# The second batch's attention state on 120 partitions instead of 80 and 40

## The chip, the core and the metric

The kernel runs on one core of one Trainium2 chip. The metric is the device time of one execution in microseconds (us), the median of several runs. Six engines matter: TensorE (PE, whose weight loads the profile lists as PEld), VectorE (DVE), ScalarE (ACT), GpSimd (POOL) and SyncE (SP), which issues most transfers.

## The reference

Three stages follow one another: a recurrent attention with gates, a dense feed-forward layer, and a feed-forward layer with 8 experts of which each token takes one. The change lies in the first.

```python
# attention: batch 2, heads 8, tokens 768, head size 40
m_new = np.maximum(f_gate[:, :, t] + m, i_gate[:, :, t])
f_stab = np.exp(f_gate[:, :, t] + m - m_new)
i_stab = np.exp(i_gate[:, :, t] - m_new)
C = f_stab[..., None, None] * C + i_stab[..., None, None] * np.einsum('bhd,bhe->bhde', vt, kt)
n = f_stab[..., None] * n + i_stab[..., None] * kt
y[:, :, t] = o * (C @ qt) / max(abs(n @ qt), 1)
# dense layer: 1536 tokens, 320 -> 2048 -> 320
h = x @ w_in;  g = np.maximum(0.01 * h, h);  x = g @ w_out
# experts: argmax of x @ w_gate picks one of 8, with room for 384 tokens each, 320 -> 1024 -> 320
```

## The kernel before

The attention is done in chunks of 128 tokens. There are 12 of them, numbered i: six (j = 0 to 5) for the first batch and six for the second, so the second batch is i = 6 to 11. Inside a chunk each token meets the others by a product of scores and values (`pi`); what came before the chunk reaches it through a state of 40 x 41 numbers a head (41: the value's 40 and the normalizer), which meets the chunk's queries in another product (`pj`). Most products run in fp16, where each operand stands as a high part and a remainder, so that the small parts are not lost.

The steps of a chunk that matter here:

- `cast` puts the queries of a head on 120 columns of `qst`: high part, low part, high part, 40 each; a transposing transfer makes `qT` of it, with these on rows 0 to 39, 40 to 79 and 80 to 119. The keys stand on 120 rows of `kT` too.
- `kw` (att_kw, L332, POOL) multiplies the chunk's keys by their decay, written twice beside each other: 128 partitions x 8 heads x 2 x 40 fp32 numbers.
- `st` (att_state) multiplies `kw` (weights, 80 columns a head, fp32) with the values: `pu`, 8 products (L343), whose 80 rows hold the same state twice. In the trace each shows as two records. POOL multiplies the old state by its decay (`cg`, L350), DVE adds (`cf`, L352; in a batch's first chunk DVE copies, L347), ACT rounds to fp16 (`ch`, L356, 80 partitions: high, high), and the remainder `cl` (L357, 40 partitions) is made by POOL in the first four chunks and by DVE after that. A batch's last chunk makes no state.
- `sc` makes the scores `pS` (L373, products of 120 rows and 128 columns), DVE multiplies them by the decay, ACT and DVE split them in high (`ah`) and remainder (`al`).
- `av` (att_av) makes `pi` (L397 to L399, three products a head, from chunk 4 on; one fp32 product a head, L395, in chunks 0 to 3) and, where the batch has a state already, `pj`: for each head one product of 80 rows (L407: q's high and low with the state's high) and one of 40 rows (L408: q's high with the remainder). DVE scales `pj` (L409) and adds `pi` (L412); `out` divides (POOL, L424) and gates (`y`, L426), ACT and DVE make the two halves of `xr`, POOL cuts a part of it (L440), and SP transposes it to `xT` (L447), the input of the dense layer.

The dense layer works in units: `h` (L586, eight products over 320 inputs, for up to 512 columns), then `t` (ACT L798, DVE L799), `gh` (ACT L800), `gl` (POOL L801), and two units later the products `px` into the 320 outputs (L590 to L592). Its units are the bulk of PE's work while the second batch's attention runs. After it the tokens are routed (`x2r`, `plg`, and so on), gathered and multiplied with the experts' weights (`xe`, `py`), which SP loads (`wa`, `wc`) and ACT and DVE split.

A table of steps (ORDER) sets the order in which the steps are written; for the second batch and the dense layer a scheduler with a model of the engines then sets the order of each engine's queue. Each engine works its queue in order. Products of the attention share two buffers of PSUM (pool psA, tag a); tiles of the attention in SBUF have two buffers each (pool a2).

## Time and profile before

| | |
|---|---|
| median of 3 runs | 424.47 us (424.04 to 424.86) |
| the profiled execution | 424.7 us |
| its span on the core | 423.0 us |
| mean granted clock of TensorE | 0.971 |
| instructions in the profile | 9186 |

The profiled execution lasted 1.7 us longer than its span (424.7 less 423.0), for what lies around the program. Times in the trace are microseconds from the span's start. In a timeline a row is the start, the duration, the engine, the line, the operation with its tiles (out<-in), partitions and shapes, the count, and in brackets the idle time ahead of it with what ended it. Products overlap in PE's pipeline, so a product's cost in a row of products is the distance from its start to the next start, not its duration. In a view of windows each stretch has its length, then busy us and count of PE, PEld, DVE, ACT and POOL, then the granted clock, the share of the DMA engines and GB/s.

### The profile page before, as it was taken

The numbers are of one execution on the slowest core, as the hardware profiler recorded it, in microseconds if no ns is written. First come the engines' busy times: TensorE is split into PE (matmuls) and PEld (weight loads), VectorE is DVE, ScalarE is ACT, GpSimd is POOL, SyncE is SP. The second block draws the span as 40 slices with busy tenths as digits, with TensorE's granted clock in tenths as the row PEclk, the third lists the DMA queues.
The fourth block names the chain that finished last, engine by engine and source line by source line (L and its number), as shares of the span: only waits on it lengthen the run. The fifth ranks groups of instructions, "written<-read, shape, count | busy, mean of one in ns | idle before, by whom it ended". The sixth has DMA issues, their size and how long they took to land. (4 is left out here: it accounts for less than half of the span.)

```text
span 423.0 us, 9186 instructions
## 1 busy us (share of the span) xinstructions
PE 367.9 (87%) x3597; PEld 286.3 (68%) x3597; DVE 300.8 (71%) x516; ACT 227.6 (54%) x440; POOL 170.8 (40%) x207
## 2 busy tenths in 40 slices
PE   0878657889799998999999999798779999789993
PEld 0767547668588875666656666595667898568882
DVE  8998999998669664877563374756689967866121
ACT  4461647427676747555355354751378966765222
POOL 4451651816446562465734373443124212222102
PEclk9999999669989999999999999999899999899999
DMA  9999999757998866099611349996197989722000
GB/s 172 218 296 233 262 246 211 126 108 154 210 191 122 176 153 135 2 240 180 152 43 32 60 158 302 303 238 195 45 218 218 312 223 347 169 63 61 33 17 19
DMA packets 146130, 70.22 MB, mean 166 GB/s; under 512 B 115666, under 2 KB 136692, under 8 KB 146080
## 3 DMA queue, kind: packets, MB, share of 16 engines
q1 hardware_dynamic: 144160, 65.44, 67.2%
q0 software_dynamic: 1920, 4.08, 2.7%
q8 instruction: 35, 0.57, 0.6%
q14 instruction: 15, 0.12, 0.1%
HBM read 43.65 MB, written 13.17 MB: 134 GB/s over the span
## 5 line engine op out<-in xcount | busy, mean ns | idle before, releaser
L586 PEld LDWEIGHTS <-pc 128*128 128x128 f16 x1728 | 117.9, 101 | 34.0 <-issue 11.5
L586 PE MATMUL h<-xT,pc 128*128 128x128 f16 (+3 forms) x768 | 99.6, 282 | 5.0 <-DMA xT<-xr 3.0
L801 POOL TENSOR_TENSOR gl<-t,gh 128x512 f16<-128x512 f32 (+1 forms) x52 | 60.0, 1155 | 63.6 <-ACT gh L800 63.4
L586 PE MATMUL h<-xe,pc 128*128 128x128 f16 x960 | 57.3, 222 | 5.5 <-PEq L940 2.0
L590 PE MATMUL px<-pc,gh 128*128 128x320 f16 x192 | 58.2, 305 | 2.1 <-ACT gh L800 2.1
L901 POOL DMA_INDIRECT out_dram<-ye,ix x24 | 26.7, 1114 | 81.1 <-ACT ye L900 80.1
L591 PE MATMUL px<-pc,gh 128*128 128x320 f16 x192 | 58.2, 305 | 0.0
L592 PE MATMUL px<-pc,gl 128*128 128x320 f16 x192 | 56.3, 306 | 0.6 <-POOL gl L801 0.6
L799 DVE SCALAR_TENSOR_TENSOR t<-h,t 128x512 f32<-128x512 f32 (+1 forms) x52 | 33.4, 644 | 30.0 <-ACT t L798 29.8
L889 DVE SCALAR_TENSOR_TENSOR hl<-h,hh 128x512 f16<-128x512 f32 x48 | 31.3, 685 | 32.4 <-ACT hh L888 32.3
L800 ACT ACTIVATE gh<-t 128x512 f16<-128x512 f32 (+1 forms) x52 | 30.9, 594 | 29.1 <-DVE t L799 28.6
L798 ACT ACTIVATE t<-h 128x512 f32<-128x512 f32 (+1 forms) x52 | 28.9, 555 | 29.5 <-PE h L586 28.9
L499 DVE SCALAR_TENSOR_TENSOR pc<-wa,pc 128x1024 f16<-128x1024 f32 (+1 forms) x36 | 36.9, 1024 | 8.9 <-ACT pc L498 6.8
L590 PE MATMUL py<-pc,hh 128*128 128x320 f16 x120 | 36.6, 305 | 3.1 <-PEq L943 2.3
L888 ACT ACTIVATE hh<-h 128x512 f16<-128x512 f32 x48 | 27.1, 594 | 21.5 <-PE h L586 20.2
L592 PE MATMUL py<-pc,hl 128*128 128x320 f16 x120 | 36.7, 306 | 1.6 <-DVE hl L889 1.5
L498 ACT ACTIVATE pc<-wa 128x1024 f16<-128x1024 f32 (+1 forms) x36 | 29.6, 863 | 15.3 <-DVE wa L483 9.0
L591 PE MATMUL py<-pc,hh 128*128 128x320 f16 x120 | 36.6, 305 | 0.0
L499 DVE SCALAR_TENSOR_TENSOR pc<-wc,pc 128x1280 f16<-128x1280 f32 x20 | 31.4, 1571 | 3.7 <-ACT pc L498 3.5
L498 ACT ACTIVATE pc<-wc 128x1280 f16<-128x1280 f32 x20 | 25.3, 1266 | 2.3 <-DVE wc L483 2.2
L590 PEld LDWEIGHTS <-gh 128*128 128x128 f16 x192 | 19.2, 100 | 10.8 <-ACT gh L800 2.6
L900 ACT ACTIVATE ye<-py,mt 128x320 f32<-128x320 f32 x24 | 12.4, 525 | 26.0 <-PE py L592 11.9
(178 smaller groups left out, 658.5 us busy)
## 6 DMA issues: line engine op xcount, KB each, us to landing
wc<-in_moe_w_dram SPq DMA_DIRECT2D x16, 640.0 KB, 6.5
wa<-in_moe_w_dram SPq DMA_DIRECT2D x16, 512.0 KB, 9.8
raw<-in_moe_w_out_dram SPq DMA_DIRECT2D x4, 1280.0 KB
scr<-zero SPq DMA_DIRECT2D x8, 588.0 KB, 4.4
raw<-in_moe_w_in_dram SPq DMA_DIRECT2D x4, 1024.0 KB
lb<-lam_d SPq DMA_DIRECT2D x8, 512.0 KB, 4.6
wa<-in_moe_w_dram SPq DMA_DIRECT2D x16, 128.0 KB
qkv<-in_k_dram SPq DMA_DIRECT2D x12, 160.0 KB, 2.9
```

Of the source, the lines that this page charges most:

```text
L498: nc.scalar.activation(hi, x, AF.Copy, scale=s)
L499: nc.vector.scalar_tensor_tensor(out=lo, in0=x, scalar=s, in1=hi, op0=ALU.mult, op1=ALU.subtract)
L586: nc.tensor.matmul(ph, lhsT=w, rhs=xT[:, x, 0:ncol], start=(m == 0), stop=(m == len(seq) - 1))
L590: nc.tensor.matmul(py, lhsT=gh, rhs=oh[:, kc, :], start=first, stop=False)
L591: nc.tensor.matmul(py, lhsT=gh, rhs=ol[:, kc, :], start=False, stop=False)
L592: nc.tensor.matmul(py, lhsT=gl, rhs=oh[:, kc, :], start=False, stop=last)
L798: nc.scalar.activation(t, ph, AF.Copy, scale=0.01 * S_G)
L799: nc.vector.scalar_tensor_tensor(out=t, in0=ph, scalar=S_G, in1=t, op0=ALU.mult, op1=ALU.max)
L800: mark[0] = nc.scalar.activation(gh, t, AF.Copy)
L801: nc.gpsimd.tensor_tensor(out=gl, in0=t, in1=gh, op=ALU.subtract)
L888: nc.scalar.activation(hh[:, to[0], to[1]], ph, AF.Relu)
L889: nc.vector.scalar_tensor_tensor(out=hl[:, to[0], to[1]], in0=ph, scalar=0.0, in1=hh[:, to[0], to[1]], op0=ALU.max, op1=ALU.subtract)
```

## The change

For the second batch the state is made three times instead of twice: `kw` holds three copies of the keys (960 numbers a partition instead of 640), a product of `pu` has 120 columns of weights instead of 80, and `cf`, `cg` and `ch` stand on 120 partitions. The remainder is written by DVE over the first 40 partitions of `ch`, so these hold remainder, high, high, against q's high, low, high in `qT`. One product of 120 rows a head then does what two did. The new function `copies` sets which chunks do this: i of 6 and more. The first batch keeps two copies and both products; the tiles are allocated for three copies in both.

```diff
--- before.py
+++ after.py
@@ -255,6 +255,7 @@
 
     NPB = 4
     NPOOL = 4
+    XB = NCH
     blocks = BLOCKS
     block_of = {i: (bi, o) for bi, tl in enumerate(blocks) for o, i in enumerate(tl)}
     xTs = {}
@@ -323,38 +324,50 @@
                                 fill=0.0, base=0, channel_multiplier=-1)
         T["dd", i] = dd
 
+    def copies(i):
+
+        return 2 if i < XB else 3
+
     def att_kw(i):
         b, j = divmod(i, NCH)
         xs = T.pop(("xs", i))
         if j == NCH - 1:
             return
-        kw = a2.tile([P, H, 2, D], F32, tag="kws", name=f"kw{i}")
-        nc.gpsimd.tensor_tensor(out=kw, in0=xs[:, 0].unsqueeze(2).to_broadcast([P, H, 2, D]), op=ALU.mult,
-                                in1=ws[:, j, b * H:(b + 1) * H].unsqueeze(2).unsqueeze(3).to_broadcast([P, H, 2, D]))
+        nr = copies(i)
+        kw = a2.tile([P, H, 3, D], F32, tag="kws", name=f"kw{i}").rearrange("p h r d -> p (h r d)")[:, 0:H * nr * D]
+        kw = kw.rearrange("p (h r d) -> p h r d", h=H, r=nr)
+        nc.gpsimd.tensor_tensor(out=kw, in0=xs[:, 0].unsqueeze(2).to_broadcast([P, H, nr, D]), op=ALU.mult,
+                                in1=ws[:, j, b * H:(b + 1) * H].unsqueeze(2).unsqueeze(3).to_broadcast([P, H, nr, D]))
         T["kw", i] = kw
 
     def att_state(i):
         b, j = divmod(i, NCH)
         if j == NCH - 1:
             return
-        pu = psA.tile([2 * D, H, D1], F32, tag="a", name=f"pu{i}")
+        nr = copies(i)
+        pu = psA.tile([nr * D, H, D1], F32, tag="a", name=f"pu{i}")
         kw = T.pop(("kw", i))
         for h in range(H):
             nc.tensor.matmul(pu[:, h, :], lhsT=kw[:, h].rearrange("p r d -> p (r d)"), rhs=T["qkv", i][:, 1, h, :],
                              start=True, stop=True)
-        cf = a2.tile([2 * D, H, D1], F32, tag="cf", name=f"cf{i}")
+        cf = a2.tile([3 * D, H, D1], F32, tag="cf", name=f"cf{i}")[0:nr * D]
         if j == 0:
             nc.vector.tensor_copy(cf, pu)
         else:
-            cg = a2.tile([2 * D, H, D1], F32, tag="cg", name=f"cg{i}")
+            cg = a2.tile([3 * D, H, D1], F32, tag="cg", name=f"cg{i}")[0:nr * D]
             nc.gpsimd.tensor_tensor(out=cg, in0=T.pop(("cf", i - 1)), op=ALU.mult,
-                                    in1=dk[0:2 * D, j, b * H:(b + 1) * H].unsqueeze(2).to_broadcast([2 * D, H, D1]))
+                                    in1=dk[0:nr * D, j, b * H:(b + 1) * H].unsqueeze(2).to_broadcast([nr * D, H, D1]))
             nc.vector.tensor_tensor(out=cf, in0=pu, in1=cg, op=ALU.add)
         T["cf", i] = cf
-        ch = a2.tile([2 * D, H, D1], F16, tag="ch", name=f"ch{i}")
-        cl = a2.tile([D, H, D1], F16, tag="cl", name=f"cl{i}")
+        ch = a2.tile([3 * D, H, D1], F16, tag="ch", name=f"ch{i}")[0:nr * D]
         nc.scalar.activation(ch, cf, AF.Copy)
-        lo_eng(i).tensor_tensor(out=cl, in0=cf[0:D], in1=ch[0:D], op=ALU.subtract)
+        if nr == 3:
+
+            cl = None
+            nc.vector.tensor_tensor(out=ch[0:D], in0=cf[0:D], in1=ch[0:D], op=ALU.subtract)
+        else:
+            cl = a2.tile([D, H, D1], F16, tag="cl", name=f"cl{i}")
+            lo_eng(i).tensor_tensor(out=cl, in0=cf[0:D], in1=ch[0:D], op=ALU.subtract)
         T["cs", i] = ch, cl
 
     def lo_eng(i):
@@ -404,6 +417,9 @@
             ch, cl = T.pop(("cs", i - 1))
             pj = psA.tile([P, H, D1], F32, tag="a", name=f"pj{i}")
             for h in range(H):
+                if cl is None:
+                    nc.tensor.matmul(pj[:, h, :], lhsT=qT[0:KST, h, :], rhs=ch[:, h, :], start=True, stop=True)
+                    continue
                 nc.tensor.matmul(pj[:, h, :], lhsT=qT[0:2 * D, h, :], rhs=ch[:, h, :], start=True, stop=False)
                 nc.tensor.matmul(pj[:, h, :], lhsT=qT[0:D, h, :], rhs=cl[:, h, :], start=False, stop=True)
             nc.vector.tensor_tensor(out=hh, in0=pj,
```

What the scheduler makes of it starts to differ about 131 us into the program, at the second batch's chunk 7 (the first of it that has a state). Three places follow. In these rows a number behind a tile's name tells its copies apart.

TensorE, in the middle of chunk 7's attention products, before (`v1h`, `v1l` are the values' high part and remainder):

```order
L397 LDWEIGHTS ah_1497
L397 MATMUL pi_1561<-v1h_189,ah_1497 128x41
L398 LDWEIGHTS ah_1497
L398 MATMUL pi_1561<-v1l_190,ah_1497 128x41
L407 LDWEIGHTS qT_1436
L407 MATMUL pj_1587<-ch_1453,qT_1436 128x41
L408 LDWEIGHTS qT_1436
L408 MATMUL pj_1587<-cl_1454,qT_1436 128x41
```

and in the changed kernel:

```order
L412 LDWEIGHTS al_1497
L412 MATMUL pi_1560<-v1h_189,al_1497 128x41
L421 LDWEIGHTS qT_1436
L421 MATMUL pj_1586<-ch_1453,qT_1436 128x41
L421 LDWEIGHTS qT_1436
L421 MATMUL pj_1586<-ch_1453,qT_1436 128x41
L421 LDWEIGHTS qT_1436
L421 MATMUL pj_1586<-ch_1453,qT_1436 128x41
```

The 16 products of two heights have become 8 of one; they stand ahead of the second half of `pi`, five and then three, where before all stood together.

TensorE, at the state of chunk 7, before:

```order
L592 LDWEIGHTS gl
L592 MATMUL px_756<-pc_804,gl 128x320
L343 MATMUL pu_1903<-qkv_1424,kw_1896 80x41 x6
L586 LDWEIGHTS pc_268
L586 MATMUL h<-xT_532,pc_268 128x256
```

and in the changed kernel:

```order
L602 MATMUL h<-xT_532,pc_804 128x256
L351 MATMUL pu_1894<-qkv_1424,kw_1887 120x41 x7
L606 LDWEIGHTS gh
L606 MATMUL px_756<-pc_804,gh 128x320
L607 LDWEIGHTS gh
L607 MATMUL px_756<-pc_804,gh 128x320
L386 LDWEIGHTS kT_1847
L386 MATMUL pS_0_1946<-qT_1848,kT_1847 128x128
```

The six and two products of the state have become one and seven, and stand ahead of 12 products `px` that came before them; the scores of chunk 8 have moved forward, to stand behind them.

ScalarE, at the exponentials of two decay matrices (`lb`, L321 before and L322 after), before:

```order
L798 ACTIVATE t<-h 128x512
L321 ACTIVATE lb_1486<-lb_1486,zt 128x128 x8
L288 ACTIVATE v1h_189<-qkv_1898 128x8x40
L800 ACTIVATE gh<-t 128x512
L321 ACTIVATE lb_2072<-lb_2072,zt 128x128 x8
L436 ACTIVATE xr_1759<-y_201,inv_all 128x320
```

and in the changed kernel:

```order
L814 ACTIVATE t<-h 128x512
L322 ACTIVATE lb_1485<-lb_1485,zt 128x128 x2
L452 ACTIVATE xr_1750<-y_201,inv_all 128x320
L289 ACTIVATE v1h_189<-qkv_1889 128x8x40
L322 ACTIVATE lb_2062<-lb_2062,zt 128x128 x8
L816 ACTIVATE gh<-t 128x512
```

A unit's `gh` stood between the two groups of eight exponentials and now stands behind both; `xr` of an earlier chunk, which stood behind both, now stands between them.

## Rows read from the trace of the kernel before

**Rows 1.** The page's first part: busy time, share and instructions of each engine.

```profile
PE 367.9 (87%) x3597; PEld 286.3 (68%) x3597; DVE 300.8 (71%) x516; ACT 227.6 (54%) x440; POOL 170.8 (40%) x207
```

**Rows 2.** Windows: busy PE, PEld, DVE, ACT, POOL, granted clock, DMA share, GB/s.

```profile
131.00:141.00 10.00, 9.73 (x137) 8.23 (x135) 9.70 (x18) 5.99 (x11) 5.14 (x6) 1.00 1.03 163
...
151.00:161.00 10.00, 9.58 (x70) 6.25 (x69) 5.42 (x9) 4.46 (x10) 5.90 (x8) 1.00 0.66 117
161.00:171.00 10.00, 8.91 (x81) 5.45 (x79) 4.41 (x9) 7.21 (x18) 3.89 (x5) 1.00 0.52 118
...
231.00:241.00 10.00, 9.44 (x92) 6.46 (x90) 3.77 (x14) 3.04 (x7) 2.79 (x4) 1.00 0.48 89
...
262.00:275.00 13.00, 10.70 (x93) 7.29 (x92) 8.30 (x10) 8.87 (x15) 4.69 (x5) 1.00 1.03 296
```

**Rows 3.** Groups of PE by line and form: the first products of pj, ten chunks.

```profile
L407 PE MATMUL pj<-ch,qT 80*128 80x41 f16 x80 | 16.0, 200 | 0.0
```

**Rows 4.** Timeline of PE at chunk 8's pi (24 products) and pj (16).

```profile
182.76 0.18 PE L397 MATMUL pi<-v1h,ah 128*128 128x41 f16 x1
...
183.34 0.18 PE L399 MATMUL pi<-v1h,al 128*128 128x41 f16 x1
183.37 0.18 PE L407 MATMUL pj<-ch,qT 80*128 80x41 f16 x1
183.48 0.19 PE L408 MATMUL pj<-cl,qT 40*128 40x41 f16 x1
183.60 0.19 PE L407 MATMUL pj<-ch,qT 80*128 80x41 f16 x1
...
185.23 0.19 PE L408 MATMUL pj<-cl,qT 40*128 40x41 f16 x1
185.35 0.60 PE L586 MATMUL h<-xT,pc 128*128 128x512 f16 x2
```

**Rows 5.** Timeline of PE at a chunk's scores, between products of 128 rows.

```profile
131.39 0.39 PE L373 MATMUL pS<-qT,kT 120*128 120x128 f16 x4
131.61 0.27 PE L586 MATMUL h<-xT,pc 128*128 128x256 f16 x1
```

**Rows 6.** Timeline of PE and PEld at fp32 products of 80 and of 128 columns.

```profile
195.54 1.27 PE L343 MATMUL pu<-qkv,kw 128*80 128x41 f32 x16
196.65 0.60 PE L586 MATMUL h<-xT,pc 128*128 128x512 f16 x2
...
68.98 1.23 PEld L343 LDWEIGHTS pu<-qkv,kw 128*80 128x80 f32 x16
70.25 0.96 PEld L317 LDWEIGHTS pb<-lam,identf 16*128 16x128 f32 x8
...
32.34 3.75 PE L395 MATMUL pi<-qkv,lb 128*128 128x41 f32 x16
35.88 0.24 PE L407 MATMUL pj<-ch,qT 80*128 80x41 f16 x1
```

**Rows 7.** Timeline of POOL at kw of chunk 8, and what follows it.

```profile
153.96 1.26 POOL L332 TENSOR_TENSOR kw<-qkv,ws 128x640 f32<-128x640 f32 x1
155.85 1.16 POOL L801 TENSOR_TENSOR gl<-t,gh 128x512 f16<-128x512 f32 x1 [0.62 <-ACT gh L800]
```

**Rows 8.** Timeline of DVE: additions on 80 and on 128 partitions.

```profile
154.96 0.48 DVE L352 TENSOR_TENSOR cf<-pu,cg 80x328 f32<-80x328 f32 x1
...
141.76 0.49 DVE L412 TENSOR_TENSOR hh<-hh,pi 128x328 f32<-128x328 f32 x1
```

**Rows 9.** Timeline of ACT, POOL, SP and PE: from chunk 7's output to its xT.

```profile
144.71 2.43 ACT L321 ACTIVATE lb<-lb,zt 128x128 f32<-128x128 f32 x8
...
146.41 0.72 POOL L424 TENSOR_TENSOR hh<-hh,dn 128x320 f32<-128x320 f32 x1
...
153.23 1.21 SPq L447 DMA_TRANSPOSE xT<-xr  x1
...
156.10 1.89 PE L586 MATMUL h<-xT,pc 128*128 128x512 f16 x8 [0.42 <-DMA xT<-xr]
```

## The prediction

> **What bounds the kernel now.** I read the page's busy times first, then windows of ten microseconds over the stretch that the change touches, then PE's timeline at the products that change, and last the chain that leads from the attention's output to PE. PE is busy for 87% of the span, ahead of DVE with 71%, ACT with 54% and POOL with 40% [rows 1]. An average could hide that PE waits just here, so the windows decide: from 120 to 262 us, where the second batch's attention runs between the dense layer's units, there are four windows in which PE isn't busy throughout, and those are shown: 0.27, 0.42, 1.09 and 0.56 us of idle time, 2.34 us in 142 [rows 2]. The granted clock is 1.00 in each of these windows, so all distances of this stretch are at the full level of 2.4 GHz. In it PE's queue itself is the limit: a microsecond taken out of it should move nearly all that follows by a microsecond. From 262 us on, where the experts begin, this ends: 10.70 of 13 us [rows 2].
>
> **What is removed: half of the products `pj`.** In chunk 8 the 16 products run from 183.37 to the next unit's `h` at 185.35, 1.98 us or 0.124 us each, without any wait [rows 4]. The 24 products `pi` just ahead of them have as many columns (41) and the same type, yet 23 distances fill 182.76 to 183.34, 0.025 us each [rows 4]. The difference isn't the size. It shows where the height changes: from `pi` (128 rows) to the first product of 80 rows 0.03, from 80 rows to 40 rows 0.11, from 40 back to 80 0.12, from the last of 40 rows to `h` with 128 rows 0.12 [rows 4]. A product of 120 rows stands between products of 128 at no such price: four scores with 128 columns take 0.22 us, from 131.39 to the next `h` at 131.61, 0.055 us each [rows 5]. So I read the 0.124 as the price of a change of height among products of 80, 40 and 128 rows, and expect none of it among 120 and 128. The new eight products then cost between 0.025 each (the pace of `pi`, same 41 columns) and 0.055 (the scores, which have three times the columns); I take 0.025, since the columns are the same. A chunk saves 1.98 less 8 x 0.025, which is 1.78; five chunks of the second batch have such products (7 to 11; the trace's 80 products of 80 rows are eight in each of ten chunks, five of these unchanged [rows 3]), so the sum is 8.9 us, and 7.7 at 0.055.
>
> The Trainium skill, "TensorEngine Tiling (Array Packing)", section "Key Properties", says that changing the tiling mode drains the engine, a change of tile within a mode not. The trace's 0.11 to 0.12 at each change of height [rows 4] agrees with it, and the unpaid step between 120 and 128 rows [rows 5] too; it bears out the reading by heights against the first rival below, whose time would be 422.4 us.
>
> **What is added on PE: wider weights for `pu`.** A product of the state has 120 columns of fp32 weights instead of 80. Each shows as two records, 16 a chunk, and 16 take 1.11 us (195.54 to 196.65), 69 ns each [rows 6]. The weight loads beside them go by columns: 16 loads of 80 columns in 1.23 us are 77 ns each, eight of 128 columns right behind them in 0.96 us are 120 ns each [rows 6], so 48 columns cost 43 ns and 40 columns 36 ns. Five chunks (6 to 10; the last makes no state) have 80 records, 2.9 us in all, on PE's path. The bounds are far apart: nothing, if the load isn't what paces them (a gain is excluded, no column is taken away), and 11.0 us, if they fell to the pace of the fp32 products of 128 columns near the program's start, 16 in 3.54 us (32.34 to 35.88) or 221 ns [rows 6], of which 120 columns are 207: 138 ns more for each of 80. I take 36 ns, because these loads, 69 us into the program, are at the pace that this stretch has, and they stand side by side.
>
> **What is added elsewhere.** POOL's `kw` has half more numbers: 1.26 us for 640 [rows 7], so 0.63 more in each of five, 3.2 us on POOL. What hides it is POOL's idle time: behind `kw` of chunk 8 it waits 0.62 us for ACT before its next `gl` [rows 7], and over the span it is busy for 40% [rows 1]. Uncovered it would delay a `gl` by up to 0.63 us a chunk, and PE has two units in hand before it needs that one. The additions and the rounding on 120 instead of 80 partitions keep their time: 0.48 us for 80 partitions, 0.49 for 128 with as many numbers in each [rows 8]. The remainder is the same instruction on DVE with another target, and the products wait for it as they did. ACT, the DMAs and their number don't change. All these are zero in the sum.
>
> **What is moved.** The scheduler's new order costs something at one place that I can name. A unit's `gh` on ACT, which stood between two groups of eight exponentials, now stands behind both, and a group takes 2.43 us [rows 9]. Behind this `gh` come its `gl` on POOL and three products for each chunk of the unit on PE. Against it, `xr` of chunk 7 has less ahead of it on ACT. The chain from chunk 7 to its transposed output is the one place in this stretch where PE waits for the attention (POOL `hh` at 146.41, SP's transfer at 153.23, PE at 156.10 after 0.42 us of idle time [rows 9]). PE will come there earlier by the 1.78 of chunk 7 less twice 0.58 for two states, 0.6 us, and can lose that and part of the exponentials' 2.43: between 0 and 2.4 us. PE works on units two behind, so I take a third, 0.8 us. The scores of chunk 8 and the state of chunk 7 come forward on PE; their inputs are made by POOL and DVE, and a stall there is within the same bounds.
>
> **The sum.** 8.9 saved, 2.9 and 0.8 added: 5.2 us less. The profiled execution, 423.0 of span and 1.7 around it, would go from 424.7 to 419.5. The median is 0.2 lower than that execution, so I predict 419.3 us.
>
> **Rivals.**
> First, the price belongs to each product of `pj`, or to its partners, not to the change of height: the new ones stay 0.124 apart. For it: no row shows a product of 120 rows with 41 columns. Against it: `pi` has the same columns at 0.025 [rows 4]. It would save 5 x 8 x 0.124, which is 5.0, less 2.9: 422.4 us.
>
> Second, the gain doesn't reach the end. From 262 us PE is busy for only 10.70 of 13 us while the DMA engines are at a share of 1.03 [rows 2]; if the experts' weights came at a time of their own, PE would wait there for what it had won, and the time would be about 424.5 us. Against it: SP issues these loads behind gates that compute opens, so they move with it.
>
> Third, slower: the wider fp32 products fall to the slow pace of the program's start. At 207 ns instead of 69 they add 11.0 us against the 8.9 saved: 2.1 more, 426.6 us. The point from which it decides is 69 + 8.9 us / 80 = 180 ns a record. For it: the same kind of product has run at such a pace in this trace [rows 6]. Against it: all five states of this batch lie in the stretch where a record takes 69 ns [rows 6].
>
> Fourth, slower too: rows cost nothing at all on PE, a removed product is worth what one of `pi` is, 0.025 us, and the rest of the 1.98 belongs to the change between `pi`'s operands and `qT`, which stays. Then 40 products save 1.0 us, the states cost 2.9, and the time is 426.4 us. Against it stands the even 0.12 from product to product inside `pj`, where the operand doesn't change [rows 4]. The Trainium skill, "TensorE: Matmul & The Clock Gate", section "LDWEIGHTS (loading the stationary operand)", states that a load's time goes by the columns and not by the rows. That speaks against this change twice, for fewer rows were no saving and more columns are a cost. The trace agrees on the columns (77 and 120 ns [rows 6]) and doesn't on the rows (0.124 against 0.025 [rows 4]).
>
> **How the numbers follow.** The forecast has 0.74, the first rival 0.09, the second 0.09, the third and the fourth 0.04 each. The forecast's own range is 416.5 to 421: 2.9 us lower if the wider weights cost nothing (416.4), and 1.6 higher if the moved `gh` costs the whole 2.4 (420.9). To hold 8 times in 10 the range takes in the first rival too: 416.5 to 422.6, which leaves out the other three with 0.17 and a little of the forecast's tails. About 0.2%, 0.85 us, is what a measurement of this kernel can tell from no change. Faster than 423.6 are the forecast and the first rival, 0.83; the second is the same, 0.09; slower are the third and fourth, 0.08.
>
> **What would show it.** In the changed trace, eight products `pj` should fill about 0.2 us with no larger step towards `pi` or `h`; 16 records of `pu` about 1.67 us instead of 1.11; `kw` on POOL about 1.9 us; and from 131 to 262 us PE should still have little idle time, perhaps more where `xT` of chunk 7 or the moved `gh` is awaited. By 262 us PE should stand about 5 us ahead of the old trace, and the experts keep that lead. I am wrong if `pj` stays at 0.12 a product, if a record of `pu` exceeds 0.18 us, or if PE's idle time between 131 and 275 us grows by more than 2 us.

## The result, and the profile after

The changed kernel takes 429.49 us (median of 4 runs, 428.25 to 431.18) against 424.46 for the kernel before, measured beside it: a ratio of 1.0137, with a 95% interval of 1.0096 to 1.0178 (the two medians alone give 1.0119; the ratios below are those on record, with their intervals). By the medians it is 5.0 us slower; 5.2 us faster was predicted. Its profiled execution lasted 430.62 us, with a span of 428.9 and a mean granted clock of 0.955.

The new instructions cost what was expected of them. Groups by line and form, of the kernel after (count, then busy us and mean ns of one, then the idle time ahead):

```profile
L421 PE MATMUL pj<-ch,qT 120*128 120x41 f16 x40 | 2.1, 181 | 0.0
L351 PE MATMUL pu<-qkv,kw 128*120 128x41 f32 x80 | 9.0, 271 | 0.0
L339 POOL TENSOR_TENSOR kw<-qkv,ws 128x960 f32<-128x960 f32 x5 | 9.8, 1957 | 0.0
```

PE's timeline after, at chunk 8's `pj` and chunk 10's `pu`:

```profile
188.16 0.18 PE L412 MATMUL pi<-v1h,al 128*128 128x41 f16 x1
188.19 0.36 PE L421 MATMUL pj<-ch,qT 120*128 120x41 f16 x8
188.39 1.67 PE L602 MATMUL h<-xT,pc 128*128 128x512 f16 x7
...
217.32 1.77 PE L351 MATMUL pu<-qkv,kw 128*120 128x41 f32 x16
218.93 0.31 PE L607 MATMUL px<-pc,gh 128*128 128x320 f16 x1
```

Eight products `pj` fill 188.19 to 188.39, 0.20 us where sixteen took 1.98 [rows 4]; no step to `pi` or `h` is dearer than another. The sixteen records of `pu` fill 217.32 to 218.93, 1.61 us, 31 ns more for each than the 69 that were read [rows 6]. So PE has about 6 us less to do, and still the program ends later. Windows over the stretches that differ show where, first of the kernel before, then of the one after (length, busy PE, PEld, DVE, ACT, POOL, granted clock, DMA share, GB/s):

```profile
131.00:161.00 30.00, 29.31 (x296) 22.76 (x294) 21.68 (x43) 19.25 (x45) 16.38 (x19) 1.00 0.82 154
161.00:180.00 19.00, 17.91 (x158) 11.29 (x155) 12.46 (x34) 11.24 (x25) 7.81 (x9) 1.00 0.28 63
180.00:235.00 55.00, 54.66 (x451) 35.96 (x450) 32.93 (x66) 27.91 (x56) 29.83 (x37) 1.00 0.56 129
...
262.00:300.00 38.00, 32.20 (x346) 23.80 (x345) 24.25 (x64) 17.69 (x32) 13.92 (x15) 0.99 0.83 222
```

```profile
131.00:161.00 30.00, 28.58 (x298) 22.80 (x298) 26.52 (x49) 21.80 (x49) 19.52 (x21) 1.00 0.90 167
161.00:180.00 19.00, 15.94 (x134) 9.51 (x133) 6.62 (x19) 8.52 (x20) 7.48 (x9) 1.00 0.23 54
180.00:235.00 55.00, 51.59 (x407) 33.17 (x405) 34.31 (x70) 25.97 (x51) 27.57 (x31) 0.94 0.52 118
...
262.00:300.00 38.00, 33.30 (x328) 24.40 (x326) 23.47 (x52) 17.88 (x31) 13.34 (x17) 0.91 0.94 261
```

Two things are new. PE waits: from 180 to 235 us it is idle for 3.41 us (55.00 less 51.59) where it was idle for 0.34, and from 131 to 180 for 4.48 instead of 1.78. And the granted clock, 1.00 and 0.99 before, is 0.94 and 0.91 in two of the stretches. PE's timeline after names the waits (in brackets the idle time and what ended it):

```profile
169.62 1.89 PE L602 MATMUL h<-xT,pc 128*128 128x512 f16 x8 [2.60 <-DVE t L815]
...
210.86 0.45 PE L608 MATMUL px<-pc,gl 128*128 128x320 f16 x1 [3.41 <-POOL gl L817]
211.10 0.47 PE L606 MATMUL px<-pc,gh 128*128 128x320 f16 x1
211.37 0.47 PE L607 MATMUL px<-pc,gh 128*128 128x320 f16 x1
...
272.37 0.31 PE L606 MATMUL px<-pc,gh 128*128 128x320 f16 x1 [1.45 <-ACT gh L816]
...
276.01 2.83 PE L602 MATMUL h<-xT,pc 128*128 128x384 f16 x9 [1.95 <-DVE t L815]
```

Behind the wait of 3.41 us the products `px` start 0.27 us apart, where they are 0.135 apart at the full clock: PE runs at 1.2 GHz instead of 2.4, and the window from 211 to 221 us has a granted clock of 0.72. The same 0.27 stands behind the wait at 276 (products at 278.62 and 278.89). POOL's timeline after shows what the wait at 210.86 was for, and SP's and ACT's the one at 272:

```profile
202.73 1.70 POOL L758 DMA_INDIRECT scr<-x2r,slot  x1 [0.19 <-issue]
...
207.80 0.98 POOL L758 DMA_INDIRECT scr<-x2r,slot  x1 [0.30 <-issue]
...
209.64 1.17 POOL L817 TENSOR_TENSOR gl<-t,gh 128x512 f16<-128x512 f32 x1
...
202.53 0.61 ACT L816 ACTIVATE gh<-t 128x512 f16<-128x512 f32 x1
...
259.19 0.39 SPq L774 DMA_DIRECT2D out_dram<-zero  x1
259.75 1.06 SPq L558 DMA_DIRECT2D wa<-in_moe_w_dram  x1
...
270.33 1.57 ACT L514 ACTIVATE pc<-wa 128x1024 f16<-128x1024 f32 x2 [2.92 <-DMA wa<-in_moe_w_dram]
```

Two further links of the program stand here. The prediction doesn't name the first, and the second only in its second rival. **The scatters**: four indirect transfers `scr`, which store the routed tokens, stand in one block on POOL's queue and hold it from 202.73 to 208.78. The `gl` that PE wants comes behind them, at 209.64, though its `gh` was there at 203.14. **The weights**: ahead of an expert's weights (`wa`) SP issues a transfer that fills the whole result with zeros (`out_dram`, 2 MB); `wa`, issued at 259.75, is there at 270.33, and ACT waits for it. Both links stand in the kernel before too. Its scatters run from 199.34 to 204.50, and the `gl` behind them ends at 206.09, 1.04 us ahead of the first product that reads it, so PE didn't wait there. At the weights it waited already, for 1.67 us. PE's and POOL's timelines before:

```profile
207.13 0.30 PE L592 MATMUL px<-pc,gl 128*128 128x320 f16 x1
...
265.95 1.46 PE L586 MATMUL h<-xT,pc 128*128 128x384 f16 x8 [1.67 <-DVE t L799]
...
204.94 1.15 POOL L801 TENSOR_TENSOR gl<-t,gh 128x512 f16<-128x512 f32 x1
```

### The profile page after: what moved, and what is told of

Same layout as the page of the kernel before. It is cut to its first block, busy times and chain, and to the rows that moved or that the text cites. A ratio compares the mean times of both kernels' runs of the same rounds, so it can differ in the third digit from the quotient of the medians.

```text
span 428.9 us, 9103 instructions
## 1 busy us (share of the span) xinstructions
PE 367.7 (86%) x3557; PEld 285.2 (66%) x3557; DVE 303.3 (71%) x516; ACT 227.7 (53%) x440; POOL 173.9 (41%) x207
## 5 line engine op out<-in xcount | busy, mean ns | idle before, releaser
L602 PEld LDWEIGHTS <-pc 128*128 128x128 f16 x1728 | 119.5, 102 | 37.8 <-issue 17.2
L602 PE MATMUL h<-xT,pc 128*128 128x128 f16 (+3 forms) x768 | 103.0, 288 | 8.0 <-DVE t L815 5.3
L606 PE MATMUL px<-pc,gh 128*128 128x320 f16 x192 | 59.3, 312 | 3.9 <-ACT gh L816 3.9
L608 PE MATMUL px<-pc,gl 128*128 128x320 f16 x192 | 57.3, 310 | 3.5 <-POOL gl L817 3.4
L607 PE MATMUL px<-pc,gh 128*128 128x320 f16 x192 | 59.6, 312 | 0.0
L606 PE MATMUL py<-pc,hh 128*128 128x320 f16 x120 | 35.9, 299 | 3.1 <-PEq L959 2.3
L607 PE MATMUL py<-pc,hh 128*128 128x320 f16 x120 | 35.9, 299 | 0.0
L608 PEld LDWEIGHTS <-gl 128*128 128x128 f16 x192 | 19.4, 102 | 11.8 <-POOL gl L817 4.2
```

What stands on the lines that cost most here:

```text
L602: nc.tensor.matmul(ph, lhsT=w, rhs=xT[:, x, 0:ncol], start=(m == 0), stop=(m == len(seq) - 1))
L606: nc.tensor.matmul(py, lhsT=gh, rhs=oh[:, kc, :], start=first, stop=False)
L607: nc.tensor.matmul(py, lhsT=gh, rhs=ol[:, kc, :], start=False, stop=False)
L608: nc.tensor.matmul(py, lhsT=gl, rhs=oh[:, kc, :], start=False, stop=last)
```

## The experiments

To tell the new instructions from their new order, most kernels below fix each engine's order, up to the experts, by ties: every instruction names the one ahead of it as a dependency that orders the queue and waits for nothing.

```diff
+            for s in steps:
+                at += s
+                for ins in [rows[e][at]] + SECOND_OF.get(rows[e][at].name, []):
+                    if last is not None:
+                        tc.add_manual_dep(ins, last, mybir.DependencyInfo(mybir.DependencyClass.NoSync, mybir.DependencyReason.DATA),
+                                          reason="place")
+                    last = ins.name
```

All ratios are to the kernel before, measured on the same chip; 0.01 is 4.2 us.

**Instructions or order?** First the changed instructions in before's order, then before's in the changed kernel's order. The edit is the ties above, with the other kernel's places.

> The changed kernel's instructions, with each engine's queue up to the experts tied to the places it has in the kernel before (an order-only tie from each instruction to the one ahead of it; in place of two products of pj stands the one). Theory 'order': the change's own instructions gain what was forecast and the loss comes from the new order of the queues; then 424.5 less 6.0 (8.9 less 2.9) and no moved gh: 418.0 to 420.0 us. Rival 'instructions': wider weights, kw or the state on 120 partitions cost more than their rows say, whatever the order; then about the changed kernel's time, 427 to 431 us. Rival 'clock': denser products or chance lower the granted clock in any order; then 422 to 427 us with a granted clock near 0.96 instead of 0.97.

> The kernel before's instructions (80 and 40 partitions, 16 products of pj a chunk), with each engine's queue up to the experts tied to the places of the changed kernel. Theory 'order': the new order's waits stay and the 6 us that the change gains are missing: 431 to 437 us. Rival 'instructions': the old instructions give the old time in any order, 423.5 to 426 us.

Measured: 1.0096 (1.0064 to 1.0128) and 1.0179 (1.0126 to 1.0232). The theory that the order alone is at fault falls, since the new instructions lose 4.1 us in the old order too. But the new order costs by itself: with the old instructions it takes 7.6 us more. The two losses don't add up to 11.7 us. The changed kernel, which has both, is at 1.0137, and in the new order the new instructions are no slower than the old ones.

**The two halves, each alone, in before's order.** The first takes the price of changing heights away and leaves `pu` as it was (its second product takes the state's high part once more, so the remainder's part is left out of the result); the second has only the wider state.

```diff
-                nc.tensor.matmul(pj[:, h, :], lhsT=qT[0:D, h, :], rhs=cl[:, h, :], start=False, stop=True)
+                hi = 2 * D if i >= NCH else D
+                two_ = nc.tensor.matmul(pj[:, h, :], lhsT=qT[0:hi, h, :], rhs=(ch if i >= NCH else cl)[:, h, :], start=False, stop=True)
```

> The kernel before in its own order; in the second batch the second product of pj takes 80 rows instead of 40 (the state's high part in place of the remainder, which leaves the remainder's part out of the result), so 16 products of one height stand where two heights alternated. If the price of 0.12 us belongs to the change of height: 16 x 0.025 + 0.12 = 0.52 us a chunk instead of 1.98, five chunks 7.3 us: 417 to 418.5 us. If it belongs to each product of pj: unchanged, 424.0 to 425.0 us. If the order theory is wrong and PE's gains don't reach the end: 423.5 to 424.5 us with the products at 0.025 in the trace.

```diff
+        nr = 2 if i < NCH else 3
...
+                one_ = nc.tensor.matmul(pj[:, h, :], lhsT=qT[0:2 * D, h, :], rhs=ch[0:2 * D, h, :], start=True, stop=False)
+                two_ = nc.tensor.matmul(pj[:, h, :], lhsT=qT[0:D, h, :], rhs=cl[:, h, :], start=False, stop=True)
```

> The kernel before in its own order, with three copies of the keys in kw, 120 columns of weights in pu and the state on 120 partitions (high, high, high) in the second batch, the remainder kept apart and both products of pj kept: the change's cost without its gain. Theory: 36 ns for each of 80 records, 2.9 us: 427 to 428 us. If the loads are hidden: 424.0 to 425.0. If the rival 'instructions' holds (kw on POOL or the wider weights delay more than their rows say): 430 us or more.

Measured: equal heights 1.0044 (1.0016 to 1.0073), wide alone 1.0072 (1.0034 to 1.0110). The second is 3.1 us, where the prediction had 2.9 for it. The first is the surprise: its sixteen products, as many as before, stand 0.025 us apart, and the steps between them and their neighbours of 128 rows are as short: 0.02 us from `pi`, 0.03 to `h`. So the price of 0.11 to 0.12 us belongs to the steps into and out of products of 40 rows, and not to any change of height. The equal heights take 1.57 us a chunk out of PE's queue (1.98 less 16 x 0.0256), 7.8 us in five, and the program gets 1.9 us longer. Its timelines, of PE at chunk 8's `pj`, of PE at a wait, and of ACT:

```profile
184.05 0.18 PE L401 MATMUL pi<-v1h,al 128*128 128x41 f16 x1
184.07 0.18 PE L409 MATMUL pj<-ch,qT 80*128 80x41 f16 x1
...
184.48 1.46 PE L592 MATMUL h<-xT,pc 128*128 128x512 f16 x6
...
207.35 0.45 PE L598 MATMUL px<-pc,gl 128*128 128x320 f16 x1 [2.61 <-POOL gl L807]
207.59 0.47 PE L596 MATMUL px<-pc,gh 128*128 128x320 f16 x1
207.86 0.47 PE L597 MATMUL px<-pc,gh 128*128 128x320 f16 x1
...
190.45 2.44 ACT L323 ACTIVATE lb<-lb,zt 128x128 f32<-128x128 f32 x8 [1.55 <-DMA lb<-lam_d]
```

ACT's timeline of the kernel before, at the same exponentials:

```profile
188.85 2.45 ACT L321 ACTIVATE lb<-lb,zt 128x128 f32<-128x128 f32 x8
```

PE comes earlier to the same `gl`, and stands. A third link shows on ACT: **the decay matrices**. `lb` of a chunk is loaded from DRAM into one of two buffers, and ACT's exponentials now wait 1.55 us for it, where they had followed without a wait. Behind them ACT, and POOL behind ACT, stay late: POOL's scatters begin at 200.05 instead of 199.34. PE is earlier and what feeds it is later. At this `gl` it can be added up: PE would be there at 204.74 (207.35 less the wait), 2.39 us earlier than in the kernel before, the `gl` ends at 207.29, 1.20 us later, and 1.04 were to spare, which makes 2.55 of the 2.61 us. SP issued that load of `lb` 0.70 us later than before (182.78 and 182.08); why, no run shows.

**Is it the scatters?** In the kernel with equal heights POOL's four scatters were moved behind later `gl`, as one block (its queue, by line):

```diff
-L748 DMA scr<-x2r_1302,slot_2409 3072x392 x4
 L612 TENSOR_SCALAR zero<-tokid 128x1
 L446 TENSOR_SCALAR xr_2676<-xr_2676 128x2x64
 L807 TENSOR_TENSOR gl<-t,gh 128x512 x2
+L430 TENSOR_TENSOR hh_2591<-hh_2591,dn_2681 128x8x40
+L807 TENSOR_TENSOR gl<-t,gh 128x512
+L748 DMA scr<-x2r_1302,slot_2409 3072x392 x4
```

> The equal-heights kernel (16 products of pj of one height, which leaves the remainder's part out), in the old order but with POOL's four scatters of the first routed block (and the two small instructions that refill their source) behind the next three gl and one hh. In its trace PE stood 2.61 us for the gl behind these scatters and then ran for a while at a lower granted clock. Theory 'second chain' (PE's gain turns into waits on a chain through the lb load, ACT, DVE and POOL, and the clock falls behind the wait): with this link shortened about 2.6 us of waiting and 1.4 us of clock come back: 1.5 to 4 us below the equal-heights kernel. Rival 'the wait only moves': within 1 us of it.

The others also have two fills of the scatter's target (`scr` with zeros) behind the last `lb` load on SP's queue, with equal heights, with before's instructions as a control, and with the changed ones:

```diff
-L768 DMA scr<-zero 128x3x392 x2
 L278 DMA lb_2494<-lam_d 128x8x128
 L208 DMA qkv_2543<-in_v_dram 128x8x40
 L208 DMA qkv_2543<-in_q_dram 128x8x40
-L768 DMA scr<-zero 128x3x392
+L768 DMA scr<-zero 128x3x392 x3
```

> As the run before, and SP's two zero fills that stand ahead of the last chunk's lb load stand behind the loads. Theory 'second chain', with the lb load as its start: another 0 to 2 us lower, 422 to 424 us where the kernel before has 424.5. Rival 'the wait only moves': like the equal-heights kernel, 0.4% above the kernel before.

> The kernel before with the same two moves, the control: PE waits for nothing there, so both theories expect the kernel before's time within 1 us.

> The changed kernel's instructions in the old order with the same two moves. Theory 'second chain': from 1.0% above the kernel before down to 0 to 0.5% above, since the wait of 2.76 us at this gl and the clock behind it go. Rival 'the wait only moves': 0.8 to 1.1% above.

Measured: 1.0020 (0.9985 to 1.0056), 1.0019 (0.9984 to 1.0054), the control 1.0048 (1.0014 to 1.0082), the change 1.0076 (1.0038 to 1.0114). Little is won. The wait at 207 is gone, but the block, whose last scatter now begins at 213.27, stands before another `gl` that PE wants; POOL and PE of the second kernel:

```profile
216.70 1.15 POOL L807 TENSOR_TENSOR gl<-t,gh 128x512 f16<-128x512 f32 x1
...
217.91 0.31 PE L598 MATMUL px<-pc,gl 128*128 128x320 f16 x1 [2.44 <-POOL gl L807]
```

The control says that a block of four at this later place costs the old kernel too. So the block has to be spread.

**Spread scatters, and a light load of `lb`.** The scatters stand as two, one and one between later `gl`, and the two fills behind `lb` as above; the changed instructions and, as a control, the old ones:

```diff
-L760 DMA scr<-x2r_1302,slot_2382 3072x392 x4
...
+L760 DMA scr<-x2r_1302,slot_2382 3072x392 x2
+L819 TENSOR_TENSOR gl<-t,gh 128x512
+L760 DMA scr<-x2r_1302,slot_2382 3072x392
+L458 TENSOR_SCALAR xr_2709<-xr_2709 128x2x64
+L819 TENSOR_TENSOR gl<-t,gh 128x512
+L760 DMA scr<-x2r_1302,slot_2382 3072x392
```

> The changed kernel's instructions in the old order, with the scatters spread and the zero fills behind the last lb load, the lb loads whole. Theory 'second chain': the wait of 2.8 us for gl and the clock behind it go and don't come back one unit later as in the run with the scatters in one block: from 1.0% above the kernel before to 0.3% above or less (chunk 7's waits stay). Rival 'the wait only moves': 0.7 to 1.1% above.

> The kernel before with the scatters spread and the fills behind, the control for the run above: both theories expect the kernel before's time within 1 us.

Two more load an eighth of `lb`, one head's row for all of them, which leaves the other heads' decay out:

```diff
-            late(nc.sync.dma_start(lb, lam_d[b * H:(b + 1) * H, j * P:(j + 1) * P].partition_broadcast(P)), "lam")
+            late(nc.sync.dma_start(lb[:, 0], lam_d[b * H, j * P:(j + 1) * P].partition_broadcast(P)), "lam")
```

> The changed kernel's instructions in the old order, with three things relieved: POOL's four scatters of the first routed block stand singly between later gl, SP's two zero fills stand behind the last chunk's lb load, and each lb load brings one head's row only (64 instead of 512 KB; all heads use it, so the decay of the others is left out), while the number of exponentials stays. Against the run below, which differs from it by the change's instructions alone: theory 'second chain' (PE waits for lb load, ACT, DVE, POOL) expects 3 to 6 us less, since the chain is short now and PE is the limit; rival 'PE's time doesn't count in this kernel, or the clock takes it' expects no gain, 0 to 4 us more.

> The kernel before with the same three things relieved, the control for the run above. Theory 'second chain': 0 to 3 us below the kernel before, whose PE hardly waits there. The rival gives no reason for a difference.

Measured: the change spread 0.9986 (0.9963 to 1.0009), the old one spread 0.9998 (0.9969 to 1.0026). With the light load 0.9912 (0.9877 to 0.9948) and 0.9929 (0.9893 to 0.9964). The change no longer loses: the two moves are worth some 4.7 us to it (1.0096 to 0.9986) and nothing to the old kernel. The load of `lb` is worth about 3 us to both, so it is a cost of the program rather than of the change. Between the two light kernels 3 to 6 us were expected and 0.7 showed, with intervals that overlap. What the change still lacks stands at the experts, in SP's, ACT's and PE's timelines of the spread kernel:

```profile
251.99 0.39 SPq L776 DMA_DIRECT2D out_dram<-zero  x1
252.54 1.06 SPq L560 DMA_DIRECT2D wa<-in_moe_w_dram  x1
...
263.54 1.06 ACT L516 ACTIVATE pc<-wa 128x1024 f16<-128x1024 f32 x1 [3.50 <-DMA wa<-in_moe_w_dram]
...
266.37 2.54 PE L604 MATMUL h<-xT,pc 128*128 128x384 f16 x8 [3.04 <-DVE t L817]
```

The same weights in the kernel before:

```profile
252.83 1.99 SPq L542 DMA_DIRECT2D wa<-in_moe_w_dram  x1
...
263.11 1.06 ACT L498 ACTIVATE pc<-wa 128x1024 f16<-128x1024 f32 x1 [2.13 <-DMA wa<-in_moe_w_dram]
```

Behind the 2-MB fill the weights land 11.0 us after their issue, and in the kernel before it was 10.3: they are issued 0.3 us earlier and are there 0.4 us later, and PE, with its lead, waits 3.04 us where it waited 1.67.

**All three places.** The result's fill moves behind the weight loads as well (SP's queue):

```diff
 L560 DMA wa<-in_moe_w_dram 128x2x512
 L561 DMA wa<-in_moe_w_dram 64x512
...
 L570 DMA wc<-in_moe_w_dram 128x4x320
+L776 DMA out_dram<-zero 128x12x320
-L776 DMA out_dram<-zero 128x12x320
```

Beside the changed kernel again as it was, this was done to the change in before's order, to the old instructions as a control, and to the change in its own order.

> The changed kernel itself, beside the runs of this call, so that order and instructions stand in one square (old and new instructions in old and new order). All theories expect its measured ratio again, 1.010 to 1.018 times the kernel before.

> The changed kernel's instructions in the old order, with the scatters spread, the two zero fills behind the last lb load, and the 2 MB zero fill of the result, which stands ahead of an expert's weight loads at 252 us, behind the later weight loads. Theory 'second chain, link by link': ACT waited 3.5 us for these weights and PE 3.0 us behind it; with the fill out of the way 1 to 3 us come back and the time is 0.3 to 0.9% below the kernel before (421 to 423.5 where that has 424.7). Rival 'the wait only moves': as the run without this third move, 0 to 0.3% below.

> The kernel before with the same three moves, the control. Theory: PE waits 1.7 us at the weights in its trace, so up to 1.5 us may come back here too: 0 to 0.4% below the kernel before; the change's own share is the difference to the run above, 2 to 5 us in its favour by the theory, 0 to 1 by the rival.

> The changed kernel in its own new order with the same three moves. Theory: the wait of 3.4 us for gl behind the scatters with the clock behind it (5 us by the milestones) goes; 1.0 to 1.8% above the kernel before becomes 0.3% above to 0.5% below; what stays is chunk 7's waits in the new order. Rival 'order alone': still 0.8% above or more.

Measured: the change again 1.0149 (1.0095 to 1.0204); relieved in before's order 419.42 us, 0.9877 (0.9831 to 0.9924); the control 0.9969 (0.9933 to 1.0004); relieved in its own order 0.9896 (0.9845 to 0.9947). With the three moves the change is 5.1 us faster than the kernel before, and has the lowest ratio of this study; the control has 1.4 of that without the change, so 3.7 us are the change's own. Windows of the relieved change in before's order:

```profile
180.00:235.00 55.00, 54.53 (x456) 36.08 (x454) 37.19 (x73) 28.72 (x59) 31.52 (x38) 1.00 0.53 129
```

From 180 to 235 us PE is busy again but for 0.47 us, at a clock of 1.00.

**One place at a time, in the change's own order.** First only the scatters spread, then only the result's fill moved.

> The changed kernel in its own new order, with the four scatters spread and nothing else moved. If the wait for gl behind them, with the clock behind it, is the larger part of the new order's loss: 4 to 6 us below the changed kernel, 0 to 0.5% above the kernel before. If the three moves share evenly: about 1.0% above.

> The changed kernel in its own new order, with the zero fill of the result behind the weight loads and nothing else moved. If the weights' link is worth what the trace shows (waits of 1.5 and 2.0 us and 2.7 us of clock behind them): 2 to 5 us below the changed kernel; if only the scatters matter: within 1.5 us of it.

Measured: 1.0040 (0.9997 to 1.0083) and 1.0002 (0.9969 to 1.0035). Against 1.0149 that is 4.6 and 6.2 us, and all moves together (0.9896) give 10.7: within their intervals (some 2 us each way) the two places add up. The windows and rows, first with the scatters spread, then with the fill moved (its last row, from the view of the DMA issues from 258 to 266 us, ends with the us from issue to landing):

```profile
180.00:235.00 55.00, 54.66 (x460) 36.44 (x459) 35.90 (x77) 29.23 (x59) 31.18 (x37) 1.00 0.54 126
...
254.29 1.06 SPq L560 DMA_DIRECT2D wa<-in_moe_w_dram  x1
...
264.82 1.58 ACT L516 ACTIVATE pc<-wa 128x1024 f16<-128x1024 f32 x2 [2.87 <-DMA wa<-in_moe_w_dram]
```

```profile
180.00:235.00 55.00, 51.65 (x428) 33.63 (x427) 34.96 (x71) 26.28 (x52) 27.78 (x31) 0.97 0.52 118
...
211.45 0.31 PE L610 MATMUL px<-pc,gl 128*128 128x320 f16 x1 [3.35 <-POOL gl L819]
...
258.68 0.37 SPq L560 DMA_DIRECT2D wa<-in_moe_w_dram  x1
...
wa<-in_moe_w_dram SPq DMA_DIRECT2D x1, 512.0 KB, 3.9
```

Each move removes its own wait and leaves the other: with the scatters spread PE is idle for 0.34 us from 180 to 235, and the weights still take 10.5 us (254.29 to 264.82); with the fill moved the wait of 3.35 us for `gl` stays, and the weights land 3.9 us after their issue; ACT turns to them at 266.81, without a wait.

## Why the prediction was wrong

The dense layer's products `px` are the same in all these kernels, so their starts are marks along PE's queue. The table is worked out from the profiled executions: how much later than in the kernel before PE passes from one mark to the next (us; the marks by their times in the kernel before).

| kernel | start to 131.0 | to 177.5 | to 202.4 | to 212.8 | to 258.1 | to 274.4 | to the end | span |
|---|---|---|---|---|---|---|---|---|
| after | +2.7 | +1.8 | -2.6 | +5.1 | -1.7 | +3.9 | -3.4 | +5.9 |
| after, scatters spread | +2.1 | +2.9 | -2.7 | -0.8 | -1.8 | +2.9 | -1.3 | +1.3 |
| after, fill moved | +2.2 | +3.0 | -2.6 | +3.9 | -1.7 | -1.7 | -2.1 | +1.0 |
| after, all relieved | +1.8 | +2.9 | -2.6 | -1.3 | -1.8 | -1.7 | +0.5 | -2.2 |
| changed, old order | +4.7 | +1.5 | -2.1 | +5.1 | -0.6 | +1.9 | -2.4 | +8.1 |
| changed, old order, all relieved | +2.0 | +1.4 | -2.4 | -0.8 | -0.9 | -2.7 | -1.5 | -5.0 |
| old, all relieved | +1.2 | +0.5 | 0.0 | 0.0 | -0.3 | -2.2 | +1.0 | +0.2 |
| old, new order | +2.2 | +3.7 | +0.4 | +4.8 | 0.0 | -0.4 | -1.0 | +9.8 |
| old, old order, scatters spread | 0.0 | +2.4 | 0.0 | 0.0 | -0.2 | +0.1 | -2.3 | -0.1 |
| equal heights, old order | -0.4 | +1.1 | -2.7 | +3.4 | -0.9 | +1.3 | +0.5 | +2.3 |

**The prices were right.** The fall from 1.98 to 0.20 us a chunk came as forecast [rows 4, 5]. The reading behind it was too wide: the step from 128 to 80 rows cost only 0.03 [rows 4], and the kernel with equal heights pays nothing between 80 and 128 either. The 0.11 to 0.12 hangs on the products of 40 rows, and since the change removes just these, the saving didn't suffer. The third and fourth rivals (fp32 at a slow pace, rows that cost nothing) and the first (0.124 stays) didn't happen. The wider weights cost 31 ns a record where 36 were taken, and 3.1 us by themselves. `kw` takes 1.96 us where 1.9 was said. The Trainium skill, "TensorE: Matmul & The Clock Gate", section "LDWEIGHTS (loading the stationary operand)", lets a load's time go by its columns and not its rows. The trace agrees for the loads, on the columns in the records of `pu` and on the rows too: at chunk 8 of the kernel before a load of 40 rows takes 0.09 us, one of 80 or 128 rows 0.10. What was dear is the distance between products and not the load, so the prediction's 0.124 against 0.025 was no test of that rule.

**The step that failed** is the one on the bound: "In it PE's queue itself is the limit: a microsecond taken out of it should move nearly all that follows by a microsecond." Between 177.5 and 202.4 us this holds: two `pj` less two `pu` are 2.4 us by the prediction's terms, and the marks come 2.1 to 2.7 us closer in every kernel with the changed instructions but the one with the light `lb`, where it is 1.2. It fails at three places:

- From 202.4 to 212.8 the change should have gained again, and loses 5.1 us to the scatters' block. With them spread the same stretch gains 0.8 to 1.3.
- From 258.1 to 274.4 it loses 3.9 us to the weights behind the fill; with the fill moved it gains 1.7 (the old instructions gain 2.2 by the moves), while spreading the scatters alone leaves a loss of 2.9.
- From 131.0 to 177.5 it should have come 0.6 us earlier, and loses 1.8 to 3.2 in its own order and 1.2 to 1.5 in the old one, relieved or not. Here lies chunk 7, whose `lb` ACT waits for: 2.26 us at its first exponentials in the kernel before, 3.60 in the relieved one in the old order. With the light load this stretch comes 0.6 earlier with the change, and 1.1 earlier with the old instructions. But the old instructions lost 2.4 here in one execution too (scatters spread, granted clock 0.94 from 131 to 161 us). A cure that leaves nothing out wasn't tried, so this part of the gain stays missing, and its cause is likely but not shown.

PE's busy share of 98% from 120 to 262 us [rows 2] showed that PE was the last to be ready at nearly every meeting. It didn't show by how much. The other chain (load of `lb`, exponentials on ACT, `gh` on ACT, scatters and `gl` on POOL) had hardly any slack, 1.04 us at the `gl` behind the scatters, so the first microsecond saved on PE used it up, and the rest became waits.

**Why a loss and not just no gain.** Rival two had the mechanism, a gain that doesn't reach the end, with 424.5 us. Its argument against was wrong: "SP issues these loads behind gates that compute opens, so they move with it". In the spread kernel PE is 0.9 us ahead at the mark of 258.1; the issue came forward by 0.3 us only and the landing not at all: 252.83 and 263.11 us before, 252.54 and 263.54 in the spread kernel. And even this rival stops at zero. Two things take the time below it. One is that the other chain comes later by itself: with equal heights PE leaves the wait for `gl` 0.22 us later than in the kernel before (207.35 and 207.13). The other is what follows a wait: the granted clock. In the window from 180 to 235 us the kernel after is idle for 3.41 us, and its 51.59 busy us at a clock of 0.94 hold, by an estimate from these two numbers, 3.1 us that the full clock would not need. So the stretch loses about as much by the slower products behind the wait as by the wait. The runs show the two together, going and coming with the wait (equal heights: a wait of 2.61 us and products 0.27 apart behind it; scatters spread: no wait, clock 1.00); no run kept the wait and the clock apart, so the share of each rests on the windows alone.

**The term for what is moved** was mis-sized as well: 0.8 us for the moved `gh`, within 2.4 at most. The old instructions in the new order take 7.6 us more than in the old, and relieved the change still takes 1.9 us more in its own order than in the old one by the medians (421.36 and 419.42, though the intervals overlap). In the trace of the kernel after, PE waits 0.77 us (at 151.88) for a `t` that stands on ACT behind the place named, the moved `gh` and its exponentials. The dearer wait of the new order is the one of 2.60 us at 169.62, for a `t` that stands on ACT (at 168.27) behind eight later exponentials, which wait for their `lb`. The old instructions in the new order wait at both places too, 1.23 and 2.96 us, and then 1.96 us for `al`, not for `gl`. ACT after, and PE with the old instructions in the new order:

```profile
165.92 2.44 ACT L322 ACTIVATE lb<-lb,zt 128x128 f32<-128x128 f32 x8 [3.02 <-DMA lb<-lam_d]
```

```profile
171.10 1.89 PE L591 MATMUL h<-xT,pc 128*128 128x512 f16 x8 [2.96 <-DVE t L804]
...
214.33 0.21 PE L401 MATMUL pi<-v1h,al 128*128 128x41 f16 x1 [1.96 <-DVE al L383]
```

**The forecast's own signs.** "If PE's idle time between 131 and 275 us grows by more than 2 us" was named as what would show the prediction wrong, and it did: from 131 to 262 us alone it grew from 2.35 to 8.53 us.

**Open.** Up to 131 us, before the orders differ, the profiled executions of the changed instructions with a whole `lb` stand 1.8 to 4.7 us behind the kernel before (the kernel after 2.7), and the others with a whole `lb` between 0.4 ahead and 2.4 behind. Of this 0.5 us is chunk 6's wider `pu`, which the new instructions have in this stretch. The rest is open: the granted clock differs (0.64 after, 0.77 before from 90 to 100 us), and the single executions don't settle whether the change has a part in that. From 131 us on the relieved change stands 7.0 us better than before and its control 1.0, a difference of 6.0 in these two executions; by the medians it is 3.7.

## What to carry to other kernels

An engine that is 98% busy and shows no waits is the last to arrive, and that says nothing of how far ahead the others are: before a saving on it is counted, look at each thing that it meets in the stretch (a tile from another engine, a load) and note how long that has been ready; the saving is worth that much (1.04 us at the `gl` here), up to the next such meeting. Blocks on a queue that nobody waits for today (four scatters in a row, a large fill ahead of loads) are the first to be met when the busy engine gets faster, so spread them or put them behind what is urgent together with the saving. To tell instructions from order, tie the order.

## What the runs showed of the hardware

Products of 120 rows among products of 128 pay nothing (eight in 0.20 us), and neither do products of 80 rows among products of 128 (sixteen in 0.41 us); only the steps between 40 rows and 80 or 128 paid 0.11 to 0.12 us each [rows 4]. An indirect transfer holds POOL for 0.98 to 1.70 us at its issue, four of them for 6 us. A load of 512 KB of weights landed 10.3 us after its issue behind a fill of 2 MB, and 3.9 us after it with the fill moved. The granted clock fell to its lower level, 1.2 of 2.4 GHz, behind waits of 3.41 and 2.61 us here, and didn't behind one of 2.60 us (at 169.62) nor behind one of 2.96 (old instructions in the new order, at 171.10), where the products that follow stay at the full clock, so the length of the wait alone doesn't tell.
